# Attention and two mixing layers on one core: where the weight conversion stands in the first layer, who clamps, and which slices use seven products

## The chip, the cores and the metric

One Trainium2 core out of the chip's eight. The time of a kernel is the device time of one execution in microseconds (us); lower is better. The kernel before was timed three times: 1032.47, 1029.22 and 1031.71 us, median 1031.71.

The engines: TensorE (PE; its weight loads PEld), VectorE (DVE), ScalarE (ACT), GpSimd (POOL), and SyncE (SP), which here issues the DMAs.

## The reference

```python
x = attention(q, k, v, M_prev, z_prev, beta)   # B=4 H=8 S=576 D=64 -> 2304 tokens x 512
h = x @ moe_w_in;  g = h - tanh(h);  x = g @ moe_w_out        # d_ff 2048
h = x @ moe2_w_in                                             # d_ff 1024
e = exp(h - max(h)); sm = e / (sum(e) + 1e-9); s = h * sm
ln = (s - mean(s)) / sqrt(var(s) + 1e-6) * g_ln
out = ln @ moe2_w_out
```

The weights of both layers arrive as 64-bit floats, which no engine here reads as such. The kernel turns each tile of weights into fp32 out of the two 32-bit words of each value.

## The kernel before

**Two-part numbers.** Each fp32 operand is kept as a high and a low part (`hi`, `lo`, both fp32r); a product of two operands is three matmuls (`ORDER`).

**Stages.** Attention runs first (to about 222 us of the span). Then MoE1: d_ff is cut into 8 slices of 256 columns, the tokens into 6 blocks of 384, which make 3 pairs. The *first mixing* runs the first two pairs (4 blocks) through slices 0 to 7. The *second part* runs the last pair through all 8 slices again, with weights that the first mixing left in DRAM as converted fp32 (`kept`). The *third stage* is Moe2, 18 tiles of 128 tokens. The accumulators `yT` stay in SBUF.

**Seven products.** A slice's first matmul on a pair of blocks is a 2 by 2 block product. `h_step` (L687) does it plainly, 24 matmuls of 384 columns for each block. `h_pair` (L726) does it for a pair with seven instead of eight block products, 42 matmuls, out of sums of the weights (`S1`..`S4`, tile `S`, made by `sums_w`, L599 to L604) and sums of the tokens (`T1`..`T4`, made once by `sums_x`). The partial products are copied from PSUM by ScalarE (L733, L735, L737) or added by VectorE. The kernel before uses seven products from slice 1 on. After the products come tanh and a subtraction, then `G`: a ScalarE cast (L754) and a GpSimd subtraction (L755). `y_step` (L768) multiplies `G` with `wo`, 24 matmuls a block; VectorE adds the result to `yT` (L781; L779 in slice 0). The Y steps of a pair follow the products of the next pair (`todo`).

**Weight units.** `Weights` converts one *unit* (128 partitions, 512 values) at a time; a slice has four: two of `wi`, two of `wo`. A unit's steps: a DMA into a `raw` buffer, ScalarE `abs` (L905), the clamp (L907, VectorE), VectorE L910, L914, L919 and L921, GpSimd's add (L923), a ScalarE cast to `hi` (L931), GpSimd's subtraction for `lo` (L933), and, in the first mixing, the DMA to DRAM. A unit of Moe2's second weight has a GpSimd scaling (L926) too. A unit that is read back from DRAM has the split alone (L931, L933). `pump` finishes the running unit up to its end and issues the next as far as its split; it is called after each Y step in the first mixing, three times after each Y step in the second part (two reloaded units and one *late* unit of Moe2's weights). `raw` has two buffers; the reloaded units have two smaller ones of their own (`raw1`), and the loader looks three units ahead there.

Order is that of the code (`manual_schedule`): each engine runs its instructions in the order in which they are issued, and waits on semaphores.

## Time and profile before

| | us |
|---|---|
| median of three runs | 1031.71 (1029.22 to 1032.47) |
| the profiled execution | 1034.89 |
| its span | 1033.1, mean granted clock 0.897 |
| PE busy | 843.2 (82%) |
| DVE busy | 635.5 (62%) |
| POOL busy | 534.0 (52%) |
| ACT busy | 399.0 (39%) |

By stage, from the trace (us from the span's start; busy time within):

| stretch | length | PE | DVE | ACT | POOL | PEclk |
|---|---|---|---|---|---|---|
| 222 to 314: slice 0 and start of slice 1 | 92 | 62.93 | 55.64 | 27.23 | 54.38 | 0.83 |
| 314 to 611: rest of the first mixing | 297 | 210.16 | 165.49 | 87.08 | 127.84 | 0.82 |
| 611 to 791: second part | 180 | 156.22 | 94.75 | 57.08 | 89.85 | 0.91 |
| 791 to 844: start of the third stage | 53 | 32.89 | 27.17 | 9.04 | 14.56 | 0.77 |

Busy times of the engines overlap. PE's busy time is that of matmuls whose ends are modelled; it is smallest against its stretch where PE waits for another engine. [...]

### The profile page before, as it was taken

To read this page: it belongs to the slowest core of one execution; us is meant where nothing else is said; L and a number is where in the kernel's file an instruction comes from. 1 tells how busy PE (TensorE), PEld (TensorE's weight loads), DVE (VectorE), ACT (ScalarE), POOL (GpSimd) and SP (SyncE) were. 2 spreads that over 40 slices of the span, in tenths; PEclk is the share of its full clock that TensorE was granted. 3 is DMA by queue.
4 is the path that set the end of the run, shared out by engine and by line. 5 is a ranking of instruction groups with operands and counts; after the bars stand their busy time and mean duration, and the time that the engine had idled before them with its cause. 6 is when DMAs were issued, how large, how long until landed. Compare 5 with 4: busy or idle time off the path is not lost.

```text
span 1033.1 us, 13383 instructions
## 1 busy us (share of the span) xinstructions
PE 843.2 (82%) x4732; PEld 723.7 (70%) x4732; DVE 635.5 (62%) x1155; ACT 399.0 (39%) x814; POOL 534.0 (52%) x504
## 2 busy tenths in 40 slices
PE   3999999985767676767676769899886589999998
PEld 1667666775757575766676769888786478888887
DVE  4999899645655555556565534565564466666663
ACT  2888888723322222232232232333332122232222
POOL 4988999858453435344443462544554214334331
PEclk8999999997888887888887789999888699999999
DMA  7587887310011111111102212233232013333341
GB/s 170 134 194 164 166 158 169 98 55 0 1 61 65 58 61 62 61 61 58 65 28 82 85 53 76 86 94 111 83 94 68 0 42 122 120 115 122 111 124 41
DMA packets 86403, 90.94 MB, mean 88 GB/s; under 512 B 51649, under 2 KB 61633, under 8 KB 86209
## 3 DMA queue, kind: packets, MB, share of 16 engines
q1 hardware_dynamic: 85952, 88.95, 30.8%
q10 hardware_dynamic: 384, 1.15, 0.5%
q8 instruction: 37, 0.61, 0.2%
q14 instruction: 30, 0.24, 0.1%
HBM read 64.37 MB, written 22.54 MB: 84 GB/s over the span
## 4 chain that ended last, share of the span: by engine, by line
PE 49%; DVE 20%; POOL 11%; ACT 9%; issue 6%; DMA 4%; SPq 1%; DVEq 0%; ACTq 0%; POOLq 0%
PE H L726 10%; PE H L976 8%; PE Y L768 6%; PE T L378 4%; POOL cvw L923 3%; PE X L402 3%; PE S L268 3%; DVE cva L910 2%; DMA raw<-in_moe_w_in_dram 2%; DVE cvw L914 2%; DVE yT L781 2%; DVE cva L921 2%; DVE cva L907 2%; DVE t L700 2%; PE H L687 2%
## 5 line engine op out<-in xcount | busy, mean ns | idle before, releaser
L768 PE MATMUL Y<-G,wo 128*128 128x384 f32 x1152 | 206.0, 336 | 1.7 <-DVE yT L779 1.6
L768 PEld LDWEIGHTS Y<-G,wo 128*128 128x128 f32 x1152 | 200.6, 188 | 2.4 <-issue 1.9
L726 PE MATMUL H<-T,S 128*128 128x384 f32 x252 | 76.8, 460 | 113.5 <-ACT S L603 50.9
L726 PEld LDWEIGHTS H<-T,S 128*128 128x128 f32 x252 | 63.3, 271 | 121.8 <-ACT S L603 52.8
L923 POOL TENSOR_TENSOR cvw<-cvw,cva 128x512 f32<-128x512 f32 x48 | 61.6, 1283 | 139.0 <-DVE cva L921 139.0
L976 PE MATMUL H<-w2i,Ys 128*128 128x512 f32 x432 | 108.8, 408 | 20.4 <-ACT Ys L1367 10.6
L976 PEld LDWEIGHTS H<-w2i,Ys 128*128 128x128 f32 x432 | 83.9, 195 | 42.1 <-POOL Ys L1368 11.0
L755 POOL TENSOR_TENSOR G<-C,G 128x768 fp32r<-128x768 f32 x28 | 51.8, 1851 | 99.4 <-ACT G L754 99.4
L687 PE MATMUL H<-xh,wi 128*128 128x384 f32 x320 | 77.7, 381 | 23.4 <-ACT wi L931 14.6
L781 DVE TENSOR_TENSOR yT<-Y,yT 128x384 f32<-128x384 f32 (+1 forms) x126 | 80.5, 683 | 21.3 <-PE Y L768 21.2
L338 POOL TENSOR_SCALAR P<-P,sm,og 128x128 f32<-128x128 f32 (+3 forms) x128 | 87.2, 691 | 6.1 <-DVE sm L329 2.6
L907 DVE TENSOR_SCALAR cva<-cva 128x512 f32<-128x512 f32 x48 | 38.7, 807 | 76.4 <-ACT cva L905 76.4
L687 PEld LDWEIGHTS H<-xh,wi 128*128 128x128 f32 x320 | 63.2, 214 | 31.1 <-ACT wi L931 17.7
L314 ACT ACTIVATE P<-sc,mx 128x128 f32<-128x128 f32 (+3 forms) x128 | 70.8, 557 | 6.4 <-DVE mx L292 6.3
L1007 POOL TENSOR_TENSOR s<-s,nhalf 128x1 f32<-128x1 f32 x18 | 10.0, 553 | 121.5 <-DVE s L1006 121.5
L700 DVE TENSOR_TENSOR t<-H,t 128x768 f32<-128x768 f32 x20 | 19.2, 958 | 77.2 <-ACT t L699 77.2
L385 ACT COPY pt<-T 128x512 f32<-128x512 f32 (+1 forms) x95 | 54.3, 607 | 29.6 <-PE T L378 29.3
L268 PE MATMUL S<-kT,qT 64*128 64x512 f32 (+3 forms) x256 | 46.7, 487 | 20.3 <-DVE kT L183 18.4
L992 ACT ACTIVATE e<-H,s 128x1024 f32<-128x1024 f32 x18 | 20.1, 1117 | 100.7 <-DVE s L987 100.7
L292 DVE CUSTOM_DVE_ANT_0 sc<-S,mask 128x128 f32<-128x128 f32 (+3 forms) x128 | 55.7, 482 | 5.0 <-PE S L268 4.7
L378 PE MATMUL T<-ident,P 128*128 128x128 f32 x320 | 47.8, 280 | 2.1 <-POOL P L338 1.9
L402 PE MATMUL X<-pt,v 128*64 128x64 f32 (+4 forms) x576 | 48.0, 319 | 0.0
(202 smaller groups left out, 1729.7 us busy)
## 6 DMA issues: line engine op xcount, KB each, us to landing
raw<-in_moe_w_in_dram SPq DMA_DIRECT2D x24, 512.0 KB, 4.0
q<-in_q_dram SPq DMA_DIRECT2D x64, 140.0 KB, 3.2
w<-cvw SPq DMA_DIRECT2D x32, 256.0 KB, 2.2
raw<-in_moe_w_out_dram SPq DMA_DIRECT2D x16, 512.0 KB, 3.6
raw<-w SPq DMA_DIRECT2D x32, 256.0 KB, 2.7
D<-rest SPq DMA_DIRECT2D x15, 512.0 KB, 2.6
rest<-D SPq DMA_DIRECT2D x60, 128.0 KB, 3.0
out_dram<-rest SPq DMA_DIRECT2D x17, 256.0 KB, 3.0
```

The lines of the kernel that those rows point to most:

```text
L268: nc.tensor.matmul(s, Q[rows, P * r : P * r + P], K[rows, 0:w], start=True, stop=True, skip_group_check=True,)
L314: self.nc.scalar.activation(t, self.sc.pop((p, i)), AF.Exp, bias=self.mx[p][:, i : i + 1], scale=-1.0, accum_out=self.sm[p][:, i : i + 1],)
L338: self.nc.gpsimd.tensor_scalar(d, d, self.sm[p][:, i : i + 1], og, ALU.mult, ALU.mult)
L378: nc.tensor.transpose(T[:, P * i : P * i + P], t, self.ident)
L402: self.nc.tensor.matmul(self.X[j * D : (j + 1) * D, q0 : q0 + w], v[:, kb, j, :], self.pt[p, gs[j]][:, at[j] : at[j] + w], start=False, st ...
L687: nc.tensor.matmul(H[:, f], wi[:, wl, c // 2 * 2 + f, c % 2], self.x[n][xl][:, c], start=(count[f] == 0), stop=(count[f] == 3 * KD - 1),)
L726: nc.tensor.matmul(to, t[:, wl, i, c], b[xl][:, c], start=(first and k == 0), stop=(k == len(steps) - 1), skip_group_check=True,)
L768: nc.tensor.matmul(Y[d][:, 0:NB], wo[:, wl, f, d * P : (d + 1) * P], G[:, gl, f], start=(i == 0), stop=(i == 3 * KF - 1),)
L781: nc.vector.tensor_tensor(y, src, y, ALU.add)
L907: nc.vector.tensor_scalar(a, a, self.LEAST, self.MOST, ALU.max, ALU.min)
L923: self.eng.tensor_tensor(w, w, a, ALU.add)
L976: nc.tensor.matmul(H[:, nh * 512 : (nh + 1) * 512], Y[:, yl, c, :], w2i[:, wl, c, nh * 512 : (nh + 1) * 512], start=(k == 0), stop=(k == 3 ...
```

## The change

- A unit's destination is allocated when its split is issued, not when it is queued. All units share the two `raw` buffers; the loader looks two units ahead everywhere. `cva` has two buffers instead of one, `cvw` three instead of two.
- Slices 0 and 1 are plain, by blocks; seven products from slice 2 on. The sums of the tokens for both pairs are made while slices 0 and 1 run, in the four rooms of `C`; `sums_w_again` is gone.
- In a pair, the running unit's end (its split, with the weight sums after the second `wi` unit) is issued after the seventh product, ahead of the tanhs, or behind a Y step where two units are under way; a new unit's fetch, `abs` and clamp are issued ahead of each `G` cast, its VectorE steps and GpSimd add inside the next Y step, before that step's last addition.
- The clamp is GpSimd's after attention, in the first mixing and in the second part.
- Second part: all eight slices are queued at once; a late unit is put one place, not two, behind the head of the queue; the fourth and fifth blocks take two late units. `y_split` of Moe2's tiles 0 and 1 stands at the start of the second part. Tile 1 is transposed directly like tile 0 (`direct`), its `t_step` one tile later.

```diff
@@ Moe1: weights of a slice
-    def _w(self, s): ...                  # wi, wo allocated when the slice is queued
+    def _wi(self, s, half):               # allocated when the split asks for it
+        if not half:
+            t = self.wp[s % 2].tile([P, 2, 4, 2, P], F32R, tag="wi", name=f"wi{s}")
+            self.w[s] = [t, None]
+        t = self.w[s][0][:, :, 2 * half : 2 * half + 2].rearrange("p w f c m -> p w c f m")
+        return t[:, 0], t[:, 1]
...
     def sums_w(self, s, a, b):
+        S = self.S[s] = self.sp.tile([P, 2, 4, 2, P], F32R, tag="S", name=f"S{s}")
...
-        nc.scalar.copy(S[:, 0], raw)
-        nc.gpsimd.tensor_tensor(S[:, 1], raw, S[:, 0].bitcast(F32), ALU.subtract)
-    def sums_w_again(self, s): ...
+        for t, hi, lo in ((raw, S[:, 0, 0:3], S[:, 1, 0:3]), (last, S[:, 0, 3], S[:, 1, 3])):
+            nc.scalar.copy(hi, t)
+            nc.gpsimd.tensor_tensor(lo, t, hi.bitcast(F32), ALU.subtract)
@@ h_pair
         product(chain, "A22", T4, False)
+        split()
...
         for i, g in enumerate(G):
+            start()
             t = C[:, 2 * i : 2 * i + 2, 1]
@@ y_step
             if d == 2:
+                between()
                 continue
@@ Weights
-        if words == 1 and self.more:
-            raw = self.more.tile([P, self.N], U32, tag="raw1", name="raw1", bufs=2)
-        else: ...
+        raw = self.pool.tile([P, 2 * self.N], U32, tag="raw", name="raw", bufs=2)[:, 0 : words * self.N]
...
-        while self.todo and len(self.raw) < self.ahead:
+        while self.todo and len(self.raw) < 2:
...
-            a = self.pool.tile([P, N], F32, tag="cva", name="cva", bufs=1)
-            w = self.pool.tile([P, N], F32, tag="cvw", name="cvw", bufs=2)
+            a = self.pool.tile([P, N], F32, tag="cva", name="cva", bufs=2)
+            w = self.pool.tile([P, N], F32, tag="cvw", name="cvw", bufs=3)
...
-            yield "v"
-            nc.vector.tensor_scalar(a, a, self.LEAST, self.MOST, ALU.max, ALU.min)
+            label, engine = self.clamp
+            yield label
+            engine.tensor_scalar(a, a, self.LEAST, self.MOST, ALU.max, ALU.min)
@@ the kernel: first mixing
-        s0 = m.sums_x(0, sums[0], [C[:, i] for i in range(4)])
...
-        m.sums_w_again(1)
...
-        for s in range(1, m.NS):
+        loader.clamp = "p", nc.gpsimd
+        for s in range(2, m.NS):
+            m.load_slice(s, True)
+        for s in range(m.NS, 2 * m.NS):
+            m.reload_slice(s)
...
+        for s in range(2):                 # slices 0 and 1 by plain matmuls, in blocks
+            for n in range(early):
+                if s or n > 1:
+                    next(sums, None)
+                    h_plain(s, n)
+                    if s and n % 2:
+                        m.sums_x_last(n // 2, C[:, 1], C[:, 3 if n == 1 else 2])
+                    for at in todo:
+                        m.y_step(*at, ps, yT)
+                    if (s, n) >= (0, 3):
+                        loader.pump()
+                    todo = [(s, n)]
+        for s in range(2, m.NS):
             for p in range(NP - 1):
-                m.h_pair(s, p, ps, C)
+                m.h_pair(s, p, ps, C, loader.finish, loader.begin)
...
-                    m.y_step(*at, ps, yT)
-                    if p == 0 and at == todo[-1]: ...   # load_slice(s + 1, True) or reload_slice
-                    loader.pump()
+                    m.y_step(*at, ps, yT, loader.middle)
+                    if len(loader.gens) > 1:
+                        loader.finish()
+                loader.middle()
@@ the kernel: second part and Moe2
-    loader.more, loader.ahead = w2p, 3
+        for i in range(2):
+            m2.y_split(i)
...
-                loader.todo.insert(min(2, len(loader.todo)), late.pop(0))
-                for _ in range(3):
-                    loader.pump()
+                items += 1
+                k = 2 if items in (4, 5) and late[1:] else min(1, len(late))
+                for _ in range(k):
+                    loader.todo.insert(min(1, len(loader.todo)), late.pop(0))
+                for _ in range(2 + k):
+                    loader.pump()
...
-        m2.y_split(0)
...
-        direct = (0, NTL - 2, NTL - 1)
-        m2.y_split(1)
+        direct = (0, 1, NTL - 2, NTL - 1)
...
-            if i == 1:
-                m2.t_step(0)
+            if i < 3:
+                m2.t_step(i - 1)
```

On ScalarE, in the pair that runs while a slice's second `wi` unit ends. `C` is the pair's work tile, `H` its products, `S` the sums of the weights. Before (the pair whose first product copy is `H_0_0_4178` uses `S_4002`):

```order
L931 CAST wi_4000<-cvw 128x2x2x128
L905 ACTIVATE cva<-raw 128x512
L931 CAST wi_4000<-cvw 128x2x2x128
L603 CAST S_4002<-sraw 128x1024
L905 ACTIVATE cva<-raw 128x512
L733 COPY C<-H_0_0_4178 128x384
L735 COPY C<-H_0_1_4179 128x384
```

After (the pair with `H_1_0_4673` still uses the sums of the slice before; `S_4629` is first read one pair later):

```order
L902 ACTIVATE cva<-raw 128x512
L752 CAST G_0_4566<-C 128x768
L902 ACTIVATE cva<-raw 128x512
L752 CAST G_1_4567<-C 128x768
L930 CAST wi_4561<-cvw 128x2x2x128
L616 CAST S_4629<-sraw 128x768
L616 CAST S_4629<-C 128x256
L729 COPY C<-H_1_0_4673 128x384
```

The casts to `S` stand ahead of a pair's first product copy in both; before, that pair needs them itself, now the next one does. Two `abs` stand ahead of the `G` casts.

On GpSimd, the same stretch of a slice. Before:

```order
L923 TENSOR_TENSOR cvw<-cvw,cva 128x512
L755 TENSOR_TENSOR G_2_4070<-C,G_2_4070 128x768
L755 TENSOR_TENSOR G_3_4071<-C,G_3_4071 128x768
L933 TENSOR_TENSOR wi_4000<-cvw,wi_4000 128x2x2x128
L923 TENSOR_TENSOR cvw<-cvw,cva 128x512
L933 TENSOR_TENSOR wi_4000<-cvw,wi_4000 128x2x2x128
L599 TENSOR_TENSOR sraw<-cvw 128x256
L600 TENSOR_TENSOR sraw<-sraw,cvw 128x256
L601 TENSOR_TENSOR sraw<-cvw 128x256
L602 TENSOR_TENSOR sraw<-cvw,sraw 128x256
L604 TENSOR_TENSOR S_4002<-sraw,S_4002 128x1024
```

After:

```order
L905 TENSOR_SCALAR cva<-cva 128x512
L753 TENSOR_TENSOR G_0_4566<-C,G_0_4566 128x768
L905 TENSOR_SCALAR cva<-cva 128x512
L753 TENSOR_TENSOR G_1_4567<-C,G_1_4567 128x768
L921 TENSOR_TENSOR cvw<-cvw,cva 128x512
L932 TENSOR_TENSOR wi_4561<-cvw,wi_4561 128x2x2x128
L611 TENSOR_TENSOR sraw<-cvw 128x256
L612 TENSOR_TENSOR sraw<-sraw,cvw 128x256
L613 TENSOR_TENSOR sraw<-cvw 128x256
L614 TENSOR_TENSOR C<-cvw,sraw 128x256
L617 TENSOR_TENSOR S_4629<-sraw,S_4629 128x768
L617 TENSOR_TENSOR S_4629<-C,S_4629 128x256
```

L905 is the clamp, now ahead of each `G` subtraction (L753); the add (L921), the `lo` of the unit (L932), the sums and the two `lo` of `S` (L617) stand behind both.

On SyncE, the loads of the second part with what each waits for (`in_moe_w_in` is a late unit, `w_` a reloaded one, `DMAHW` other DMAs). Before:

```order
L849 DMA raw_5685<-w_1_3533 128x512 [waits DMAHW6_49,Pool_49]
L849 DMA raw<-in_moe_w_in_dram 128x1024 [waits DMAHW4_49,DVE_49]
L849 DMA raw_5702<-w_2_3646 128x512 [waits DMAHW0_49,Pool_49]
L849 DMA raw_5767<-w_3_3692 128x512 [waits DMAHW1_49,Pool_49]
L849 DMA raw<-in_moe_w_in_dram 128x1024 [waits DMAHW7_49,DVE_49]
L849 DMA raw_5849<-w_0_3801 128x512 [waits DMAHW3_49,Pool_49]
```

After:

```order
L846 DMA raw<-w_1_3414 128x512 [waits DMAHW7_49,DMAHW1_49,Pool_49]
L846 DMA raw<-w_2_3503 128x512 [waits DMAHW0_49,DVE_49,Activation_49]
L846 DMA raw<-in_moe_w_in_dram 128x1024 [waits DMAHW1_49,Pool_49]
L846 DMA raw<-w_3_3583 128x512 [waits DMAHW2_49,Pool_49]
L846 DMA raw<-w_0_3649 128x512 [waits DMAHW3_49,DVE_49,Activation_49]
L846 DMA raw<-in_moe_w_in_dram 128x1024 [waits DMAHW4_49,Pool_49]
```

Before, a late unit's load waits for VectorE's last read of an earlier late unit, and the reloaded units for GpSimd's last read of earlier reloaded ones. Now the late unit's load waits for GpSimd's last read of a reloaded unit, and one reloaded unit for a late one.

## Rows read from the trace of the kernel before

**Rows 1.** Page's costliest groups: busy us, mean ns; then idle before and releaser.

```profile
L726 PE MATMUL H<-T,S 128*128 128x384 f32 x252 | 76.8, 460 | 113.5 <-ACT S L603 50.9
```

**Rows 2.** Timeline of PE, one slice: start, us, what [idle before <-releaser].

```profile
338.75 8.51 PE L768 MATMUL Y<-G,wo 128*128 128x384 f32 x48
...
347.09 0.91 PE L726 MATMUL H<-xh,wi 128*128 128x384 f32 x4
...
356.84 1.01 PE L726 MATMUL H<-T,S 128*128 128x384 f32 x2 [8.49 <-ACT S L603]
...
385.05 2.29 PE L726 MATMUL H<-T,S 128*128 128x384 f32 x6 [7.05 <-ACT C L733]
...
401.50 0.92 PE L726 MATMUL H<-xh,wi 128*128 128x384 f32 x4
```

**Rows 3.** Chain of waits in order of time, end of slice 0: start, us.

```profile
313.44 4.17 PE Y L768 x24
...
325.90 3.73 DMA raw<-in_moe_w_in_dram
```

**Rows 4.** GpSimd's groups of one shape each, whole span.

```profile
L923 POOL TENSOR_TENSOR cvw<-cvw,cva 128x512 f32<-128x512 f32 x48 | 61.6, 1283 | 139.0 <-DVE cva L921 139.0
...
L933 POOL TENSOR_TENSOR wi<-cvw,wi 128x512 fp32r<-128x512 f32 x16 | 21.5, 1345 | 5.1 <-ACT wi L931 5.1
...
L651 POOL TENSOR_TENSOR C<-xh,xT 128x768 f32<-128x768 f32 x4 | 8.1, 2055 | 5.1 <-DMA xT_later<-x 5.1
...
L926 POOL TENSOR_SCALAR cvw<-cvw,gl 128x512 f32<-128x512 f32 x8 | 5.6, 694 | 0.8
...
L600 POOL TENSOR_TENSOR sraw<-sraw,cvw 128x256 f32<-128x256 f32 x7 | 5.1, 724 | 0.6
...
L205 POOL TENSOR_SCALAR f<-qT 128x576 f32<-128x576 f32 x2 | 3.3, 1652 | 0.1
```

**Rows 5.** Timeline of GpSimd, first row after attention.

```profile
222.68 6.25 POOL L651 TENSOR_TENSOR C<-xh,xT 128x768 f32<-128x768 f32 x3 [5.09 <-DMA xT_later<-x]
```

**Rows 6.** Timeline of all engines, VectorE beside a running GpSimd.

```profile
344.05 1.85 POOL L755 TENSOR_TENSOR G<-C,G 128x768 fp32r<-128x768 f32 x1 [0.38 <-ACT G L754]
...
345.15 1.03 DVE L907 TENSOR_SCALAR cva<-cva 128x512 f32<-128x512 f32 x1 [1.06 <-ACT cva L905]
```

**Rows 7.** Timeline of VectorE in attention.

```profile
23.71 0.45 DVE L205 TENSOR_SCALAR f<-qT 128x576 f32<-128x576 f32 x1
```

**Rows 8.** Timeline of all engines, one block of the second part.

```profile
672.79 0.67 ACT L905 ACTIVATE cva<-raw 128x512 f32<-128x512 f32 x1
...
675.08 0.42 DVE L907 TENSOR_SCALAR cva<-cva 128x512 f32<-128x512 f32 x1
...
677.18 0.69 DVE L921 SCALAR_TENSOR_TENSOR cva<-raw,cva 128x512 f32<-128x512 uint32 x1
...
679.27 0.62 ACT L931 CAST w2i<-cvw 128x512 fp32r<-128x512 f32 x1 [5.80 <-POOL cvw L923]
...
681.21 1.28 POOL L933 TENSOR_TENSOR wi<-raw,wi 128x512 fp32r<-128x512 f32 x1
...
689.88 0.62 ACT L931 CAST w2i<-cvw 128x512 fp32r<-128x512 f32 x1 [5.80 <-POOL cvw L923]
```

**Rows 9.** DMA issues of the second part: KB each, median us to landing.

```profile
raw<-in_moe_w_in_dram SPq DMA_DIRECT2D x8, 512.0 KB, 4.0
```

**Rows 10.** Timeline of SyncE in the second part.

```profile
717.41 1.78 SPq L849 DMA_DIRECT2D raw<-in_moe_w_out_dram  x4
```

**Rows 11.** Timeline of PE, start of the second part and of the third stage.

```profile
611.53 1.14 PE L687 MATMUL H<-xh,wi 128*128 128x384 f32 x4 [0.59 <-ACT wi L931]
...
801.28 1.22 PE L976 MATMUL H<-w2i,Ys 128*128 128x512 f32 x2 [10.56 <-ACT Ys L1367]
...
809.05 7.82 PE L976 MATMUL H<-w2i,Ys 128*128 128x512 f32 x22 [6.56 <-POOL Ys L1368]
...
843.55 5.77 PE L976 MATMUL H<-w2i,Ys 128*128 128x512 f32 x24
```

More of the change, by code (lines that the diff above doesn't have):

```diff
@@ L590, in load_slice, with reload_slice @@
             )
-        for c in range(KF):
+        for c in range(self.KF):
             r = s * FS + c * P
-            self.loader.add(wo[:, 0, c, :], wo[:, 1, c, :], self.w_out[r : r + P, :], then=then)
+            self.loader.add(lambda c=c: self._wo(s, c), self.w_out[r : r + P, :], then=then)
+    def reload_slice(self, s):
+        for i in range(2 + self.KF):
+            self.loader.add(
+                lambda i=i: self._wi(s, i) if i < 2 else self._wo(s, i - 2),
+                lambda i=i: self.kept[s - self.NS][i],
+            )
     def sums_w(self, s, a, b):
-        nc, S = self.nc, self.S[s]
+        nc = self.nc
+        S = self.S[s] = self.sp.tile([P, 2, 4, 2, P], F32R, tag="S", name=f"S{s}")
         a, b = (w.rearrange("p (c f m) -> p f c m", c=2, f=2) for w in (a, b))
-        raw = self.sraw
+        raw, last = self.sraw[s > 2]
         nc.gpsimd.tensor_tensor(raw[:, 0], a[:, 1], b[:, 1], ALU.add)
@@ L601, in sums_w @@
         nc.gpsimd.tensor_tensor(raw[:, 2], a[:, 0], a[:, 1], ALU.subtract)
[L602 to L625 removed]
+        nc.gpsimd.tensor_tensor(last, b[:, 0], raw[:, 1], ALU.subtract)
+        for t, hi, lo in ((raw, S[:, 0, 0:3], S[:, 1, 0:3]), (last, S[:, 0, 3], S[:, 1, 3])):
+            nc.scalar.copy(hi, t)
+            nc.gpsimd.tensor_tensor(lo, t, hi.bitcast(F32), ALU.subtract)
     def split_x(self, n, pool, x):
@@ L823, in __init__, with add, fetch_one @@
         self.nc, self.pool = nc, pool
-        self.more, self.ahead = None, 2
-        self.todo, self.raw, self.gen = [], [], None
-        self.eng = nc.gpsimd
-    def add(self, hi, lo, src, scale=None, then=None):
-        self.todo.append((hi, lo, src, scale, then))
-    def _fetch(self):
-        hi, lo, src, *rest = self.todo.pop(0)
+        self.todo, self.raw, self.gens = [], [], []
+        self.clamp = "v", nc.vector
+    def add(self, dest, src, scale=None, then=None):
+        self.todo.append((dest, src, scale, then))
+    def fetch_one(self):
+        if not self.todo:
+            return
+        dest, src, *rest = self.todo.pop(0)
+        if callable(src):
+            src = src()
         parts = src if isinstance(src, list) else [src]
         words = parts[0].shape[-1] * (parts[0].shape[1] if len(parts[0].shape) == 3 else 1) // self.N
-        if words == 1 and self.more:
-            raw = self.more.tile([P, self.N], U32, tag="raw1", name="raw1", bufs=2)
-        else:
-            raw = self.pool.tile([P, 2 * self.N], U32, tag="raw", name="raw", bufs=2)
-            raw = raw[:, 0 : words * self.N]
+        raw = self.pool.tile([P, 2 * self.N], U32, tag="raw", name="raw", bufs=2)[:, 0 : words * self.N]
         if words == 1:
@@ L849, in _fetch, with begin, middle, finish @@
             self.nc.sync.dma_start(out=rv[i * n : (i + 1) * n], in_=part)
[L850 removed]
+        self.raw.append((dest, raw, words, *rest))
     def fetch(self):
[L854 to L859 removed]
+        while self.todo and len(self.raw) < 2:
+            self.fetch_one()
     def step(self, first):
         if first and self.raw:
[L864 to L869 removed]
+            gen = self._convert(*self.raw.pop(0))
+            next(gen)
+            self.gens.append([gen, ""])
+        if self.gens and next(self.gens[0][0], None) is None:
+            self.gens.pop(0)
+    def begin(self):
         self.fetch()
         if self.raw:
[L872 removed]
+            words = self.raw[0][2]
+            gen = self._convert(*self.raw.pop(0))
+            at = next(gen)
+            while at == "a" or at == "p" and words > 1:
+                at = next(gen)
+            self.gens.append([gen, at])
+    def middle(self):
+        for g in self.gens:
+            if g[1] != "a, split":
+                while g[1] != "a, split":
+                    g[1] = next(g[0])
+                break
+    def finish(self):
+        if self.gens:
+            for _ in self.gens.pop(0)[0]:
+                pass
     def pump(self):
         self.finish()
[L877 to L894 removed]
+        self.begin()
+        self.middle()
+    def _convert(self, dest, raw, words, scale, then):
         nc, N = self.nc, self.N
```

175 lines of the change are left out of this document (62 added, 113 removed).

## The prediction

> **What bounds the kernel now.** I read the page's groups first, for the line before which TensorE idles longest; then TensorE's timeline through one slice; then the rows of the engine that each wait names; last the loads of the second part.
>
> The first row to see is the seven products' line: 76.8 us busy, but 113.5 us of idle ahead of it, most put down to ScalarE's cast to `S` [rows 1]. One slice's timeline shows how. Y steps run without a gap, 48 matmuls from 338.75 to 347.09, so 0.174 us a matmul. Then six matmuls of the next slice run and TensorE waits 8.49 us for the `S` cast, and in the second pair 7.05 us for a product's copy (L733) that stands behind the unit's work on ScalarE. The slice takes 401.50 - 347.09 = 54.4 us [rows 2], where its 180 matmuls (2 x 42 + 4 x 24) at 0.174 are 31.3. So in the first mixing the conversion, begun late, sets the time, and TensorE's own work is not the bound. In the second part the unit chain and TensorE are close together: a block's period is 10.61 us from `w2i` cast to `w2i` cast [rows 8], its 48 matmuls 8.4. At the start of the third stage TensorE waits 10.56 and 6.56 us for `Ys` [rows 11].
>
> The change touches all four stretches. I keep the profiled execution's scale (1034.9, span 1033.1) and subtract 3.2 at the end to come to the runs' median 1031.7.
>
> **The clamp on GpSimd.** It falls in every stretch, so its price comes first. No row shows GpSimd doing a maximum and a minimum in one pass. Lower bound: its scaling of the same 128x512 with two multiplications, 0.69 us. Nearest row for a maximum: 1.65 us for 128x576, times 512/576 = 1.5 us. Upper bound: two such passes, 2.9 us [rows 4]. I take 1.5, the row with the same operation. Less than 0.69 is excluded, since no GpSimd row of this size is shorter.
>
> VectorE does that maximum in 0.45 us [rows 7] and GpSimd takes 1.65, 3.7 times as long. [...]
>
> **Slices 0 and 1, to the end of slice 2's first products.** Before, the first products with seven end and the Y step begins at 313.44 [rows 3]. Now slice 1 is plain, so `sums_w_again` goes, and the sums for both pairs are made meanwhile. GpSimd runs through from 222.68 [rows 5]: ten sums of the 2.06 us kind and four `lo` parts of that size, 29; four clamps at 1.5, four adds at 1.28, three weight `lo` at 1.35, the sums for `S` (4 x 0.72 and some 2.4 for `lo`), together 20 [rows 4]. That is 50 us of work, and about 25 us of waits for the VectorE steps between clamp and add (four chains of 2.34 to 3.3, and the casts between): it ends near 298. An `S` cast, the abs and a product copy bring TensorE's third product to about 301, and five products (5.3) with a slow start end near 308. Against 313.4: **-5**. The Y steps then due are one fewer, which is counted below.
>
> **The pairs of slices 2 to 7.** Before, from 313.4 to the second part's first matmul at 611.53 less its 0.59 us wait [rows 3, 11]: 297.5. Now the sums `S` are written one pair before they are read, so the 8.49 us wait should go. What is late next?
>
> In a pair with `S` I walk from the start of its Y steps (t = 0). The second `G` cast stands at 4.4, since `G` has three buffers and the first Y step frees one. GpSimd's queue is: clamp to 3.35, first `G` subtraction (1.85 [rows 6]) to 5.2, clamp to 6.7, second subtraction to 8.6, add to 9.9, `lo` to 11.8, four sums to 14.7. ScalarE's two `S` casts end at 15.2, and only then comes the next pair's first product copy, queued behind them, to 15.6. TensorE has waited since its second product; five products remain (30 matmuls, 5.3): a period of 21.0.
>
> In a pair without `S` the queue is shorter, but VectorE's conversion now stands ahead of a Y step's last addition. VectorE's clamp took 1.03 us beside a running GpSimd subtraction [rows 6] and 0.42 in the clear [rows 8]; I expect its 128x512 steps to be held likewise, so that the addition reads its PSUM bank at 8.6 instead of 6.3. The next Y step stalls 2.3 us, and matmuls after a stall run slowly for a while: six took 2.29 us after the 7.05 us wait [rows 2], against 6 x 0.174 = 1.05. Period 20.1. The work alone (42 + 48 matmuls) is 15.7.
>
> From the first Y step there are eleven periods: five at 21.0, five at about 20.2, a last one without conversion at 16.5: 222.5, and a last pair of Y steps 8.4: 231. Against 297.5: **-66**. The second unit's `then` stores and the two-buffer `raw` are covered in this stretch: one load of 4 us in a 20 us period.
>
> **The second part.** Before, from 610.9 to the end of the work that precedes the third stage's first wait, 801.28 - 10.56 = 790.7 [rows 11]: 179.8. The two `raw1` buffers go. Now a late unit's load waits for GpSimd's last read of a reloaded unit, as the loads' order shows, where before it waited for VectorE's read of an earlier late unit and was covered. With it the block has a ring: ScalarE's cast of the reloaded unit, GpSimd's `lo` of the late unit before it and its own (0.62 + 2 x 1.28 [rows 8]) make the release at 3.25; the load, 4.0 [rows 9]; abs 0.67; clamp 1.5; four VectorE steps 2.34 (675.08 + 0.42 to 677.18 + 0.69) [rows 8]; then VectorE's and ScalarE's steps on the block's `h` that stand between, 0.96 + 0.84. Sum 13.6, against 10.61. For Moe2's second weight, whose loads are four DMAs that take 1.78 us to issue [rows 10], and whose scaling takes 0.69 [rows 4], 14.8. Blocks with two late units go twice around, less what overlaps: 20.9. With three single blocks (40.8), two double (41.8), seven of 14.8 (103.6) and the last blocks without late units (22.5): 208.7; and the first matmuls wait for the reloaded weights to about 22 us after the stage's start. Together 231, **+51**. If the load were hidden, the periods would be 10.2 and 10.4, and this term 0; that is the lower end.
>
> **Start of the third stage.** Before, from 790.7 to the fourth tile's products at 843.55: 52.9 [rows 11]. Tiles 0 and 1 have their `Ys` ready long before, so the waits of 10.56 and 6.56 go; tile 1's direct transposes stall TensorE for some 4 us; the conversion that runs on into this stretch before is done by then. 72 matmuls of 0.24 (5.77 us for 24), a Y step of 4.2, the transposes and that stall: 31. **-22**.
>
> Sum: -5 - 66 + 51 - 22 = -42. So 1034.9 - 42 = 993 profiled, 990 on the median's scale.
>
> **The rivals.**
>
> *The load is hidden in the second part* (the loader's look-ahead puts it early enough). For it: SyncE has nothing else to do there. Against: the wait on GpSimd's read in the order itself. Term +51 becomes 0: 939. Chance 0.12.
>
> *VectorE isn't held by GpSimd in the pairs.* For it: the 1.03 us of the held clamp is a single reading, and the longer sums may be spread. Then pairs without `S` take 16.5 and those with it 20: 5 x 3.6 + 5 x 1.0 = 23 less, 967. Chance 0.12.
>
> *A cheap clamp*, 0.69 as the multiplications: 0.8 less in each of 14 rings (11), about as much in each pair with `S`, where GpSimd's queue binds (4; in the others the held addition binds), and in slice 1 (1): 16 less, 974. Chance 0.10. [...]
>
> *A dear clamp, slower than before.* If maximum and minimum are two passes, 2.9 us, the clamp's 1.4 us more comes once in each late unit's ring (16 units, +22), twice in each pair's GpSimd queue (10 pairs, +29) and four times in slice 1 (+6): +57, 1047. It decides from a clamp of about 2.4 us on. For it: the row's maximum alone costs 1.65 where two multiplications cost 0.69, so the operation, not the bytes, sets its price. Against: nothing shows that a second operation costs as much again. Chance 0.16.
>
> *The change doesn't do what it says*: ScalarE still holds the product copies, since `S` casts and unit casts still stand ahead of one (the order shows it). If both pairs then wait as the 7.05 us wait did, periods are 25: 10 x 4.5 = 45 more, 1035. Chance 0.07.
>
> **How the numbers follow.** The forecast has the remaining 0.43, with a range of its own from 965 to 1020 (a few us in each of ten periods and fourteen rings). The range 940 to 1045 holds it and all rivals between, with the first and the dear clamp at its edges, about half of each left out: some 0.14. A measurement of this kernel can tell about 0.3%, 3 us, from no change. Faster: 0.43 + 0.12 + 0.12 + 0.10 and a little of the last rival, 0.02: 0.79. Within 0.3%: the rest of the last rival and a clamp near the break-even, 0.04. Slower: 0.17.
>
> **What would show it.** Right: no wait of TensorE for an `S` cast at a slice's first pair, pair periods near 20 to 21 us, waits there put down to a product copy on ScalarE or to VectorE's addition; GpSimd's clamp near 1.5 us; in the second part `w2i` casts 13 to 14 us apart with SyncE's loads beginning after a reloaded unit's `lo`; TensorE's first two tiles of the third stage without a wait for `Ys`. Wrong: a clamp row far from 1.5; `w2i` casts still 10 us apart; Y steps back to back at 0.174 in pairs without `S`; or weights and sums that come late in slice 2, which would put the first pair of products well past 308 us.

## The result and the profile after

The changed kernel takes 999.3 us (median of four, 995.71 to 999.9) against 1031.4 (1029.22 to 1032.47): ratio 0.968, 95% interval 0.966 to 0.971. It is faster by 32 us. The profiled execution took 995.71 us, span 993.9, granted clock 0.935. Between the two profiled executions the span fell by 39.2 us. The profiled execution of the kernel after is the fastest of its four, and that of the kernel before, 1034.9, was slower than all four timed ones, so 7 of these 39 us are not in the medians.

From the page after, TensorE's costliest group:

```profile
L766 PE MATMUL Y<-G,wo 128*128 128x384 f32 x1152 | 242.9, 373 | 107.4 <-DVE yT L780 88.1
```

The idle time that stood before the seven products [rows 1] is down to 25 us for their line, now called L722. Instead 107.4 us stand before the Y matmuls, 88.1 of them released by VectorE's addition to `yT` (L780); some 68 of the 107 lie in the second part.

TensorE's timeline in one slice after (to be read against [rows 2]). A period runs from the start of one pair's Y steps to the start of the next pair's. The period from 352.68 has the `S` casts in it (*a pair with `S`*), the one from 375.34 has not (*a pair without `S`*).

```profile
352.68 6.43 PE L766 MATMUL Y<-G,wo 128*128 128x384 f32 x36
361.51 3.75 PE L766 MATMUL Y<-G,wo 128*128 128x384 f32 x12 [2.40 <-DVE yT L780]
...
369.96 1.32 PE L722 MATMUL H<-T,S 128*128 128x384 f32 x6 [2.43 <-ACT C L729]
...
375.34 6.42 PE L766 MATMUL Y<-G,wo 128*128 128x384 f32 x36
384.14 2.35 PE L766 MATMUL Y<-G,wo 128*128 128x384 f32 x12 [2.39 <-DVE yT L780]
...
393.74 6.41 PE L766 MATMUL Y<-G,wo 128*128 128x384 f32 x36
```

The 8.49 us wait for the `S` cast is gone. Pairs follow at 375.34 - 352.68 = 22.7 and 393.74 - 375.34 = 18.4 us, 41 us a slice where it was 54.4. In both periods the Y steps stop for 2.4 us after 36 matmuls, and the products that come behind the `S` casts wait 2.43 us more for their first copy (L729).

The rows of all engines in the second period show how GpSimd's running `G` subtraction holds VectorE (to be read against [rows 6]):

```profile
378.89 1.84 POOL L753 TENSOR_TENSOR G<-C,G 128x768 fp32r<-128x768 f32 x1
378.96 2.06 DVE L908 TENSOR_SCALAR cva<-cva 128x512 uint32<-128x512 uint32 x1 [0.59 <-POOL cva L905]
...
380.69 2.26 POOL L905 TENSOR_SCALAR cva<-cva 128x512 f32<-128x512 f32 x1
381.05 0.98 DVE L912 SCALAR_TENSOR_TENSOR cvw<-raw,cva 128x512 uint32<-128x512 uint32 x1
...
382.07 0.43 DVE L917 TENSOR_SCALAR cva<-cvw 128x512 uint32<-128x512 uint32 x1
382.53 0.69 DVE L919 SCALAR_TENSOR_TENSOR cva<-raw,cva 128x512 f32<-128x512 uint32 x1
...
383.13 1.88 DVE L780 TENSOR_TENSOR yT<-Y,yT 128x768 f32<-128x768 f32 x3
```

VectorE's L908, 0.43 us in the clear (at 662.79 in the second part), takes 2.06 beside GpSimd's `G` subtraction. The addition that frees the PSUM bank (L780) starts at 383.13, and TensorE goes on at 384.14, in the row shown above. L908 begins 0.07 us after GpSimd's 1.84 us subtraction and ends 0.3 us after it. The clamp did not hold VectorE so: while it ran on GpSimd from 380.69 for 2.26 us, VectorE's L912, L917 and L919, two of them with two SBUF inputs, took 0.98, 0.43 and 0.69 us, against 0.69, 0.43 and 0.69 in the second part, where no GpSimd operation ran beside them.

GpSimd's clamp in the whole span:

```profile
L905 POOL TENSOR_SCALAR cva<-cva 128x512 f32<-128x512 f32 x40 | 79.9, 1998 | 70.8 <-ACT cva L902 70.7
```

1.998 us is the mean; in the second part, where VectorE waits for it, a clamp takes 1.92. The single maximum of 128x576 took 1.65 [rows 4], so about 1.5 for 512 columns, and the minimum adds some 0.4 to it; both figures are estimates from these rows. VectorE's clamp took 0.42 [rows 8]; GpSimd's 1.92 is 4.6 times that.

One block of the second part after (to be read against [rows 8]):

```profile
652.31 0.61 ACT L930 CAST w2i<-cvw 128x512 fp32r<-128x512 f32 x1
...
654.50 1.29 POOL L932 TENSOR_TENSOR wi<-raw,wi 128x512 fp32r<-128x512 f32 x1
...
655.82 1.74 SPq L846 DMA_DIRECT2D raw<-in_moe_w_out_dram  x4
...
660.09 0.66 ACT L902 ACTIVATE cva<-raw 128x512 f32<-128x512 f32 x1 [5.98 <-DMA raw<-in_moe_w_out_dram]
...
660.84 1.92 POOL L905 TENSOR_SCALAR cva<-cva 128x512 f32<-128x512 f32 x1 [3.79 <-ACT cva L902]
...
662.79 0.43 DVE L908 TENSOR_SCALAR cva<-cva 128x512 uint32<-128x512 uint32 x1 [7.60 <-POOL cva L905]
...
667.31 0.62 ACT L930 CAST w2o<-cvw 128x512 fp32r<-128x512 f32 x1 [0.45 <-POOL cvw L924]
...
668.70 6.25 PE L766 MATMUL Y<-G,wo 128*128 128x384 f32 x24 [6.08 <-DVE yT L780]
```

The load of a late unit (SyncE, 655.82) begins when GpSimd's `lo` of a reloaded unit ends (654.50 + 1.29 = 655.79). ScalarE's abs waits 5.98 us for it; clamp, VectorE's steps and the cast at 667.31 follow. From cast to cast the block takes 15.0 us here and 14.5 to 14.9 in the next six, which all convert Moe2's second weight (`w2o`); TensorE waits 6.08 us. Blocks with a single unit of the first weight (`w2i`) take 13.5 to 14.1, where they took 10.61 [rows 8]. For `w2o` the kernel before took 11.4:

```profile
744.54 0.62 ACT L931 CAST w2o<-cvw 128x512 fp32r<-128x512 f32 x1 [6.60 <-POOL cvw L926]
...
755.94 0.62 ACT L931 CAST w2o<-cvw 128x512 fp32r<-128x512 f32 x1 [6.59 <-POOL cvw L926]
```

TensorE from the end of the pairs to the third stage's tiles, to be read against [rows 11]:

```profile
543.65 1.57 PE L682 MATMUL H<-xh,wi 128*128 128x384 f32 x8
```

```profile
774.36 5.76 PE L975 MATMUL H<-w2i,Ys 128*128 128x512 f32 x24
...
800.40 1.94 PE L1045 MATMUL T<-ident,rest 128*128 128x128 f32 x8 [4.02 <-DVE rest L1013]
...
809.39 5.75 PE L975 MATMUL H<-w2i,Ys 128*128 128x512 f32 x24
...
820.56 4.83 PE L975 MATMUL H<-w2i,Ys 128*128 128x512 f32 x20
```

The two waits for `Ys` of [rows 11] are gone, and with them a third, of 3.27 us at 824.78, that the kernel before had for tile 1. The 4.02 us wait ahead of tile 1's direct transposes is there.

| stretch | before | forecast | after |
|---|---|---|---|
| end of slice 2's first products | 313.4 | 308 | 309.6 |
| from there to the second part | 297.5 | 231 | 234.0 |
| second part to its end | 179.8 | 231 | 230.7 |
| from there to the fourth tile's products | 52.9 | 31 | 35.0 |
| the rest of the span | 189.6 | 189.6 | 184.5 |

The rows of after are 309.64, 543.65, 774.36, 809.39 and the span. The first line holds 1.5 us by which attention ended earlier. The rest of the span gained 5 us, for which the forecast had nothing. Nearly all of it comes up to the fifth tile's products, which began 15.6 us behind the fourth's before (859.17) and 11.2 after (820.56).

### The profile page after: what moved, and what is told of

Same layout as the page of the kernel before. It is cut to its first block, busy times and chain, and to the rows that moved or that the text cites. A ratio compares the mean times of both kernels' runs of the same rounds, so it can differ in the third digit from the quotient of the medians.

```text
span 993.9 us, 13377 instructions
## 1 busy us (share of the span) xinstructions
PE 830.2 (84%) x4752; PEld 718.8 (72%) x4752; DVE 637.2 (64%) x1112; ACT 397.1 (40%) x812; POOL 600.7 (60%) x540
## 4 chain that ended last, share of the span: by engine, by line
PE 40%; POOL 23%; DVE 15%; issue 8%; DMA 6%; ACT 6%; SPq 2%; ACTq 0%; DVEq 0%; POOLq 0%
PE H L975 9%; POOL cva L905 7%; PE H L722 5%; POOL cvw L921 4%; PE S L268 4%; PE T L378 3%; PE X L402 3%; DMA raw<-in_moe_w_in_dram 3%; POOL wi L932 3%; PE Y L766 3%; DVE cva L908 3%; DVE cvw L912 2%; DMA raw<-in_moe_w_out_dram 2%; DVE cva L919 2%; POOL G L753 2%
## 5 line engine op out<-in xcount | busy, mean ns | idle before, releaser
L766 PE MATMUL Y<-G,wo 128*128 128x384 f32 x1152 | 242.9, 373 | 107.4 <-DVE yT L780 88.1
L766 PEld LDWEIGHTS Y<-G,wo 128*128 128x128 f32 x1152 | 231.1, 215 | 115.3 <-ACT wi L930 49.5
L908 DVE TENSOR_SCALAR cva<-cva 128x512 uint32<-128x512 uint32 x48 | 46.9, 977 | 126.0 <-POOL cva L905 126.0
L905 POOL TENSOR_SCALAR cva<-cva 128x512 f32<-128x512 f32 x40 | 79.9, 1998 | 70.8 <-ACT cva L902 70.7
L975 PE MATMUL H<-w2i,Ys 128*128 128x512 f32 x432 | 103.7, 395 | 0.0
L921 POOL TENSOR_TENSOR cvw<-cvw,cva 128x512 f32<-128x512 f32 x48 | 62.8, 1309 | 57.8 <-DVE cva L919 57.8
L780 DVE TENSOR_TENSOR yT<-Y,yT 128x384 f32<-128x384 f32 (+1 forms) x126 | 80.5, 681 | 11.9 <-PE Y L766 11.7
L682 PEld LDWEIGHTS H<-xh,wi 128*128 128x128 f32 x384 | 67.1, 188 | 1.4 <-issue 1.4
L722 PE MATMUL H<-T,S 128*128 128x384 f32 x216 | 46.5, 358 | 25.1 <-ACT C L729 25.1
L902 ACT ACTIVATE cva<-raw 128x512 f32<-128x512 f32 x48 | 32.0, 667 | 70.8 <-DMA raw<-in_moe_w_out_dram 41.7
L722 PEld LDWEIGHTS H<-T,S 128*128 128x128 f32 x216 | 40.7, 201 | 27.0 <-ACT C L729 27.0
L991 ACT ACTIVATE e<-H,s 128x1024 f32<-128x1024 f32 x18 | 20.1, 1116 | 94.2 <-DVE s L986 94.2
L753 POOL TENSOR_TENSOR G<-C,G 128x768 fp32r<-128x768 f32 x24 | 45.6, 1901 | 10.2 <-ACT G L752 10.2
```

The costliest lines, as they stand in the source:

```text
L682: nc.tensor.matmul(H[:, f], wi[:, wl, c // 2 * 2 + f, c % 2], self.x[n][xl][:, c], start=(count[f] == 0), stop=(count[f] == 3 * KD - 1),)
L722: nc.tensor.matmul(to, t[:, wl, i, c], b[xl][:, c], start=(first and k == 0), stop=(k == len(steps) - 1), skip_group_check=True,)
L766: nc.tensor.matmul(Y[d][:, 0:NB], wo[:, wl, f, d * P : (d + 1) * P], G[:, gl, f], start=(i == 0), stop=(i == 3 * KF - 1),)
L780: nc.vector.tensor_tensor(y, src, y, ALU.add)
L905: engine.tensor_scalar(a, a, self.LEAST, self.MOST, ALU.max, ALU.min)
L908: nc.vector.tensor_scalar(au, au, 0x0FFFFFFF, 3, ALU.bitwise_and, ALU.logical_shift_left)
```

## Experiments

All are timed against the kernel before, which took 1033.3 to 1034.0 us (medians) beside them. Stretches are read from TensorE's timeline of each: *pairs*, from the first Y step after a pair to the second part's first matmul; *second*, from there to the third stage's first product; *slice*, two consecutive periods, as the mean over four slices. Up to the second part e2 has the code of the changed kernel, and slice 2's first products ended at 311.5 us in its profiled execution and at 309.6 in the other, so 2 us between single profiled executions mean nothing.

| kernel | us | ratio, 95% interval | pairs | slice | second |
|---|---|---|---|---|---|
| after | 999.3 | 0.966 to 0.971 | 234.0 | 41.0 | 230.7 |
| e1 one more buffer for reloaded units | 961.1 | 0.928 to 0.932 | 237.5 | 42.0 | 189.6 |
| e2 clamp on VectorE, second part | 977.4 | 0.943 to 0.956 | 234.1 | 41.0 | 207.4 |
| e3 addition first | 998.2 | 0.964 to 0.969 | 233.1 | 41.8 | 233.4 |
| e4 clamp on VectorE everywhere | 979.9 | 0.945 to 0.952 | 239.3 | 42.6 | 207.8 |
| e5 before, with early `Ys` | 1021.4 | 0.986 to 0.991 | as before | | 179.0 |
| e6 `S` casts later | 992.5 | 0.958 to 0.962 | 227.1 | 39.9 | 233.8 |
| e7 e3 and e6 | 987.2 | 0.953 to 0.957 | 223.5 | 39.7 | 233.2 |
| e8 e1, e2, e3 and e6 | 919.3 | 0.888 to 0.894 | 221.8 | 39.8 | 159.7 |
| e9 no clamp in the pairs | 969.3 | 0.936 to 0.940 | 233.5 | 41.7 | 209.1 |
| e10 as e8, but `cvw` of three, `Ys` room, clamp on VectorE everywhere | 899.0 | 0.867 to 0.873 | 211.8 | 37.5 | 159.0 |
| e11 as e10, but clamp on GpSimd in the pairs, split after the copies | 942.6 | 0.909 to 0.914 | 216.2 | 38.3 | 196.9 |
| e12 as e10, split after the copies | 938.2 | 0.903 to 0.912 | 216.7 | 38.3 | 195.2 |

### The second part: e1 and e2

**e1.** Every second reloaded unit gets a buffer of its own, so that late units follow each other in one `raw` buffer; `cvw` gives up a buffer for the room.

```diff
+        self.odd ^= words == 1
+        if self.more and words == 1 and not self.odd:
+            raw = self.more.tile([P, self.N], U32, tag="raw1", name="raw1", bufs=1)
+        else: ...
-            w = self.pool.tile(..., tag="cvw", name="cvw", bufs=3)
+            w = self.pool.tile(..., tag="cvw", name="cvw", bufs=2)
```

> Theory (the second part runs on a ring through the shared raw buffer: release by GpSimd, then the 4 us load, then the conversion): with a buffer of its own for every second reloaded unit, a late unit's load waits for an earlier late unit only, the block's period falls from 14.7 to about 10.7 us, the second part from 230.7 to 180 to 185, and the time from 999 to about 950. Rival (GpSimd's longer queue with the clamp sets the period, the load is beside it): the second part stays above 220 and the time above 990. cvw has two buffers here, which may cost a few us in the pairs of the first mixing.

Measured: 961 us, second part 189.6, which is 4.6 us above the forecast's 185 and far below the rival's 220. The pairs took 3.5 us more, which the expectation had allowed for the lost `cvw` buffer. One block in the second part:

```profile
651.67 0.62 ACT L935 CAST w2o<-cvw 128x512 fp32r<-128x512 f32 x1 [0.47 <-POOL cvw L929]
...
653.82 0.69 ACT L907 ACTIVATE cva<-raw 128x512 f32<-128x512 f32 x1 [0.48 <-DMA raw<-in_moe_w_out_dram]
...
656.24 1.92 POOL L910 TENSOR_SCALAR cva<-cva 128x512 f32<-128x512 f32 x1
...
662.73 0.62 ACT L935 CAST w2o<-cvw 128x512 fp32r<-128x512 f32 x1 [0.47 <-POOL cvw L929]
```

The abs waits 0.48 us for the load instead of 5.98, and casts are 11.06 us apart, less than the 11.4 of the kernel before. This shows the load's place in the ring. What is left in the ring is the clamp, which stands in GpSimd's queue behind three `lo` subtractions and starts at 656.24, 1.7 us after the abs has ended.

**e2.** `loader.clamp = "v", nc.vector` from the start of the second part.

> Theory (the clamp stands in the ring of the second part with its full length): VectorE's 0.42 in place of GpSimd's 1.92 us takes 1.5 us from each of the 16 late units: second part 230.7 - 24 = 207, time about 975. Rival (the load alone sets the ring, the clamp is hidden beside it): at most 5 us less, time above 993.

Measured: 977 us; the second part fell by 23.3 us to 207.4, as forecast. With the load in the ring, the clamp's full difference of 1.5 us counts in each of the 16 late units.

### The pairs: e3, e4, e6, e7 and e9

**e3.** `between()` after the last addition of a Y step instead of ahead of it.

> Theory (the conversion ahead of a Y step's last addition makes the next Y step wait 2.4 us for its PSUM bank in every pair): with the addition first, the pairs without S fall from 18.4 to about 16 us and those with S from 22.6 to 20 or 21, together some 20 us, time about 979. Rival (the conversion then ends later, and the unit's split or the S sums hold the next products by as much): no change, 999 within 5.

Measured: 998.2, no change; the rival holds. The wait moved:

```profile
393.92 8.48 PE L766 MATMUL Y<-G,wo 128*128 128x384 f32 x48
...
404.80 0.62 ACT L930 CAST wi<-cvw 128x512 fp32r<-128x512 f32 x1 [5.68 <-POOL cvw L921]
...
409.60 0.83 ACT L616 CAST S<-sraw 128x768 fp32r<-128x768 f32 x1 [4.19 <-POOL sraw L613]
...
411.17 2.29 PE L722 MATMUL H<-T,S 128*128 128x384 f32 x6 [6.65 <-ACT C L729]
```

The Y steps run 48 matmuls in one piece, but the product copy L729 stands on ScalarE behind the unit's cast (404.80) and the `S` casts (from 409.60), which now come later; TensorE waits 6.65 us for it. Pairs without `S` take 17.3, those with it 24 us.

**e4.** `loader.clamp` stays VectorE's.

> Theory (GpSimd's queue binds the pairs with S, VectorE's held conversion those without): with the clamp on VectorE everywhere, GpSimd has 4.2 us less in each pair, so pairs with S fall by about 3.5 us, pairs without S rise by about 1 us, and the second part falls by 24 as with the clamp moved there alone: time about 962. Rival (VectorE, held by GpSimd's running operation, becomes the bound of the pairs): pairs 2 us longer each, time about 995.

Measured: 980 us, within the spread of e2's executions (974 to 988). In the profiles the pairs take 5 us more than in e2, slices 42.6. Pairs with `S` did not get shorter (22.5 against 22.6). The rival's direction was right, with 0.8 us a pair in place of 2.

**e6.** ScalarE's `S` casts, and the subtractions behind them, are issued after the third product copy.

```diff
         nc.scalar.copy(c12, chain)
+        if self.later:
+            self.later()          # the casts to S and GpSimd's lo
```

> The changed kernel with ScalarE's S casts behind the third product copy in place of ahead of the first. Theory (in pairs with S the second wait of TensorE, 2.43 us for the copy L729, comes from the S casts ahead of it, and goes): pairs with S 22.6 to 20, five times 2.5, time about 987. Rival (the unit's cast just ahead of them holds the copy as long): pairs with S unchanged, 999.

Measured: 992.5. Pairs with `S` fell to 20.0 as forecast, but those without rose from 18.4 to 20.7 in most slices, so a slice gained 1.1 us and not 2.5.

**e7.** e3 and e6 together.

> Both edits, the addition first and the S casts later. Theory (with the addition first, the wait only moved to the copy behind the S casts, 6.65 us; with these casts later it has nowhere to go): pairs without S 17.3 as with the addition first alone, pairs with S from 24.2 to about 17, the stretch of the pairs 234 to about 200, time about 966. Rival (GpSimd's queue, some 19 us of work in a pair with S, is full): pairs with S stay at 19 to 20, time about 977.

Measured: 987, a gain of 12 us where 33 were forecast. Pairs with `S` take 17.3, the next ones 22. The rows of such a next pair, and the busy times (PE, PEld, DVE, ACT, POOL) of the stretch ahead of its cast:

```profile
381.62 0.62 ACT L941 CAST wo<-cvw 128x512 fp32r<-128x512 f32 x1 [7.59 <-POOL cvw L932]
...
382.15 0.47 ACT L737 COPY C<-H 128x384 f32<-128x384 f32 x1
...
382.68 2.29 PE L730 MATMUL H<-T,S 128*128 128x384 f32 x6 [3.73 <-ACT C L737]
```

```profile
363.06:381.59 18.53, 15.23 (x86) 14.59 (x84) 14.88 (x19) 6.47 (x11) 18.45 (x14) 1.00 0.22 69
```

The copy now waits for the unit's cast, which waits for GpSimd's add (380.33 to 381.59). GpSimd is busy 18.45 of the 18.53 us up to there: the sums' `lo` run later, and what stands behind them is late in the next pair. So here GpSimd's queue is full, as the rival said, though in the pair after the one that it named.

**e9.** The clamp left out from the pairs, the second part as in e2.

> The changed kernel with the clamp left out from the pairs of the first mixing, so that this part of the conversion isn't computed there, and on VectorE in the second part (to be read against the run with VectorE's clamp in the second part, 977 us). Theory (GpSimd's queue sets the pairs: 80 per cent busy there, two clamps of 1.9 and 2.3 us in each): pairs with and without S fall by 2 to 4 us, a slice's two pairs from 41 to about 36, time about 952. Rival (VectorE's steps, held while GpSimd runs, set them): a slice's two pairs stay above 39.5, time above 968.

Measured: 969.3, slices 41.7: the rival. GpSimd's busy time with the clamp (the changed kernel) and without it, in some two slices each:

```profile
352.70:434.70 82.00, 67.55 (x361) 65.62 (x360) 62.82 (x81) 30.53 (x53) 64.18 (x44) 0.96 0.22 77
```

```profile
350.00:432.00 82.00, 68.33 (x350) 66.42 (x350) 61.76 (x78) 29.00 (x51) 49.24 (x36) 0.92 0.23 77
```

Columns: length, then busy time of PE, PEld, DVE, ACT and POOL. GpSimd fell from 64 to 49 us of 82, and the pairs did not follow: those with `S` fell from 22.7 to 21.8, and those without rose from 18.4 to 18.8 or more. In a pair with `S`:

```profile
350.63 2.22 DVE L913 SCALAR_TENSOR_TENSOR cvw<-raw,cva 128x512 uint32<-128x512 uint32 x1
...
355.63 1.27 POOL L922 TENSOR_TENSOR cvw<-cvw,cva 128x512 f32<-128x512 f32 x1 [1.09 <-DVE cva L920]
```

GpSimd's add now waits for VectorE, whose step of 0.69 us takes 2.22 beside a `G` subtraction. So taking load off GpSimd alone brings little in the changed kernel's pairs, since VectorE's chain stands close behind. Against e2 the run gained 8 us; in the profiles 5 to 7 come from slices 0 and 1, where slice 2's first products end at 304.6 instead of 311.5 (309.6 in the changed kernel).

### The start of the third stage: e5

The kernel before with `y_split(0)` and `y_split(1)` ahead of the second part, and tile 1 in `direct`.

> The kernel before with one part of the change alone: Ys of tiles 0 and 1 written ahead of the second part, and tile 1 transposed directly. Theory (the waits of 10.56 and 6.56 us for Ys at the start of the third stage go, less some 4 us for tile 1's direct transposes): from the end of the second part to the fourth tile's products 52.9 falls to about 31, time 1032 - 22 = 1010. Rival (the conversion that still runs on into this stretch holds the tiles as well): 52.9 to 45 or more, time above 1023.

Measured: 1021.4, 12 us faster than before: half of what was expected, and just short of the rival's range (above 1023).

```profile
788.80 5.76 PE L976 MATMUL H<-w2i,Ys 128*128 128x512 f32 x24
800.06 7.09 PE L768 MATMUL Y<-G,wo 128*128 128x384 f32 x24 [5.50 <-DVE yT L781]
...
833.22 5.77 PE L976 MATMUL H<-w2i,Ys 128*128 128x512 f32 x24
```

From 788.80 to the fourth tile it takes 44.4 us. The waits for `Ys` are gone, but the Y step after tile 0 waits 5.50 us for an addition behind the late units, whose conversion still runs on into this stretch (the last `w2o` cast comes at 817.26). In the changed kernel that cast comes at 765.30, ahead of the stretch, which takes 35.0. So early `Ys` alone do not bring the forecast's gain; an early end of the conversion alone was not run.

### Together: e8, e10, e11 and e12

**e8.**

> All that helped together: addition first, S casts later, a buffer of its own for every second reloaded unit (cvw with two buffers), and VectorE's clamp in the second part. Theory (the second part is then bound by TensorE, since neither load nor GpSimd's queue is in the ring): second part near 155, pairs near 200, time 890 to 905. Rival (another ring in the second part, through GpSimd's lo subtractions and add, at 10 us a block): second part 175 to 185, time about 925.

Measured: 919, above the forecast's 905: second part 159.7 (forecast 155), but pairs 221.8 where 200 was forecast. e7 shows the same for the pairs (223.5).

**e10.** e8 with `cvw` back at three buffers, the idle third room of `Ys` as the reloaded units' buffer, and VectorE's clamp everywhere.

> Addition first, S casts later, cvw with three buffers, a room of Ys as the buffer of every second reloaded unit in the second part, and VectorE's clamp everywhere after attention. Read against the run with all that helped (919). Theory (GpSimd's queue sets the pairs, and with the addition first VectorE is no longer in TensorE's way): a slice's two pairs from 39 to 35, time about 895. Rival (VectorE held by GpSimd gives it back as it did with the clamp on VectorE alone): two pairs 40 or more, time about 925.

Measured: 899, the fastest; slices 37.5, between the theory's 35 and the rival's 40. Up to the second part e10 differs from e7 in the clamp alone: slice 2's first products end at 304.6 instead of 309.3, and the pairs take 211.8 instead of 223.5. So VectorE's clamp helps here by 16 us up to the second part, where in the pairs of e4 it cost 5. What is different here is that the addition and the product copies are out of its way, and that GpSimd's queue, which it shortens, was full (e7). VectorE is busy 87% of some two slices, and GpSimd's add waits for it:

```profile
340.00:418.00 78.00, 67.63 (x376) 65.04 (x377) 68.10 (x91) 31.67 (x55) 52.90 (x38) 1.00 0.26 86
```

```profile
371.62 1.27 POOL L937 TENSOR_TENSOR cvw<-cvw,cva 128x512 f32<-128x512 f32 x1 [2.33 <-DVE cva L935]
```

The clamp thus accounts for most of the 20 us against e8. The third `cvw` buffer shows no gain by itself: with GpSimd's clamp the pairs take 221.8 us with two buffers (e8) and 223.5 with three (e7).

**e11, e12.** The running unit's cast behind a pair's second product copy.

```diff
         nc.scalar.copy(c22, both)
+        copied()                  # loader.finish() where two units are under way
```

> As the run with all that helped, with cvw of three buffers and the room of Ys, and with the running unit's cast behind a pair's second product copy in place of ahead of its first. Theory (TensorE's remaining wait of 1.3 to 3.8 us in each pair is the first product copy behind that cast, which waits for GpSimd's add): it goes, 2 us in each of 11 pairs, a slice's two pairs from 39 to 35, time about 890. Rival (GpSimd's queue is full, the wait comes back elsewhere): two pairs above 38, time about 910.

> Both of the two before it. Theory (copies and GpSimd's queue both out of the way, 90 matmuls of 0.174 us a pair remain, 15.7): two pairs of 32 to 34, time about 875. Rival (VectorE held by GpSimd): two pairs above 37, time about 905.

Measured: 943 and 938, both worse than e10, for a reason that no theory named: the second part is back at 197 and 195 us. (e12 differs from e10 in this edit alone.) One block of e11:

```profile
638.40 1.77 POOL L949 TENSOR_TENSOR wi<-Ys,wi 128x512 fp32r<-128x512 f32 x1 [0.18 <-ACT wi L947]
...
640.19 0.34 SPq L863 DMA_DIRECT2D Ys<-w  x1
640.71 2.66 SPq L863 DMA_DIRECT2D raw<-in_moe_w_out_dram  x4
...
646.25 0.66 ACT L919 ACTIVATE cva<-raw 128x512 f32<-128x512 f32 x1 [6.86 <-DMA raw<-in_moe_w_out_dram]
```

By the code, two units are still under way when the second part starts, since no pair follows whose copies would let the first be finished; each split then runs one place later in its block. The late unit's load (640.71) now stands on SyncE right behind the load into the `Ys` room, which waits for that room's `lo` (638.40 + 1.77), and the abs waits 6.86 us for it. No run moved that load alone, so this cause is read from the rows and not tested. The pairs themselves gained little with GpSimd's clamp (38.3 a slice against 39.7 in e7), and with VectorE's they lost 0.8 us a slice (38.3 against 37.5).

## Why the prediction was right

**The sum.** It gave 993 on the profiled execution's scale; the profiled execution took 995.7. The median lies 9.3 us above the 990 that was written. Of these, 6.8 come from carrying the profiled execution's offset to the median over from the kernel before, where the median lies 3.2 below, to a kernel where it lies 3.6 above. That the sum came so near is partly luck. Its parts missed by up to 10 us and cancelled: pairs with `S` +10.2 in all, pairs without -6.3, the first stretch +1.6, the third stage +4.0, and -5.1 in the rest of the span, which had no term.

**Slices 0 and 1** (-5): 309.6 against 308, or 311 with attention's earlier end taken out. That GpSimd's queue sets this stretch, as the walk had it, is borne out by e9: without the clamps it ends 5 to 7 us earlier.

**The pairs** (-66): the stretch took 234.0 against 231. The first steps of the walk were right: the wait for `S` goes, and the next things that are late are the product copy behind the `S` casts, and the Y step behind the held conversion. Two sizes were wrong. Pairs with `S` took 22.6 (the first 24.7) against 21.0:

```profile
399.11 2.25 POOL L905 TENSOR_SCALAR cva<-cva 128x512 f32<-128x512 f32 x1
...
409.43 0.83 ACT L616 CAST S<-sraw 128x768 fp32r<-128x768 f32 x1 [4.24 <-POOL sraw L613]
```

In this one, from 393.74, GpSimd works through its queue in the order of the walk, with one gap of 0.73 us from its first clamp at 395.41 to 410.08. But its two clamps take 1.92 and 2.25 us in place of 1.5 each, and the four sums 3.4 in place of 2.9, so the `S` casts end 16.8 us after the start of the Y steps and not 15.2. The Y stall of 2.4 us comes in these pairs too, where the walk had none, but it is covered by this queue: behind it TensorE waits again, 2.43 us, for the copy. Pairs without `S` took 18.4 (the last 21.2) against 20.2. The stall is as forecast (2.4 against 2.3), but the matmuls behind it were not slow there (12 in 2.35 us at 384.14, against 3.75 at 361.51). Besides, the terms written for this period, 15.7 of work, 2.3 of stall and 1.2 for slow matmuls, give 19.2; the other 0.9 of its 20.1 has no row.

What the walk did not see is how close the next chain stands. Without the clamps, GpSimd's add waits for VectorE's held steps, and pairs with `S` still take 21.8 (e9). With the addition and the `S` casts out of the way, GpSimd's queue fills the next pair (e7). Addition, casts and clamp had to go together before the pairs fell to 18.8 (e10). What holds e10's pairs, 3 us above TensorE's own 15.7, no run tested; in its rows the first product copy stands behind the unit's cast, the cast behind GpSimd's add, and the add waits 2.33 us for VectorE.

**The second part** (+51): 230.7 against 231, and the mechanism is shown by e1 (load out of the ring: -41) and e2 (clamp out of the ring: -23). Sizes were off and cancelled. In the block shown above, the clamp costs 1.92 and not 1.5, and the release 3.5 and not 3.25. The load takes 4.3, where the forecast had 4.0 and, to come to 14.8, some 0.5 more for its four DMAs. From the end of VectorE's steps to the cast it is 2.2, where the forecast's terms give 2.5 (0.96 + 0.84 + 0.69).

**The third stage** (-22): the gain to the fourth tile was 17.9. The waits for `Ys` went, as forecast, but the sum counted 72 matmuls where 96 stand in this stretch (the first output's 24, L1074, are missing), and the parts that it names, with two transposes of 1.0 us each, come to some 27.5 and not to 31. With the missing 24 they come to 33. That the gain up to the fifth tile is 22 (68.5 before, 46.2 after) is luck. e5 shows that early `Ys` alone bring 8.5 to the fourth tile.

**The rivals.** The hidden load did not come; e1 comes nearest to it, and it took 961 where 939 was put, with GpSimd's clamp in the ring. VectorE unheld did not come: L908 shows the hold, 2.06 us in place of 0.43. The cheap clamp did not come, nor did the dear one: 1.92 lies near the middle of the bounds, 0.69 and 2.9, and below the break-even of 2.4. ScalarE did hold the product copies in pairs with `S`, but for 2.43 us and not for 7.05, and the periods of 25 did not come.

## What to carry to other kernels

Price a change by stretches and look in each for the ring that sets the period; here a gain of 64 us in one stretch hid a loss of 51 in another, and one more buffer of 2 KB per partition gave 41 of it back. Before buffers are merged, follow each load to the read that releases its buffer, and to what stands ahead of it on the queue that issues it. Where a wait is covered by a second one, taking away either alone may bring little or nothing (e3, e6, e9): take both, and look again at the engine behind them.
